# Retention and an ELU feed-forward on one core: w_out loaded in pieces of two rows, strided FFN1 weights, and w_in's last quarter moved ahead of w_out

## The chip, the cores and the metric

The kernel runs on one core of one Trainium2 chip. The metric is the device time of one execution in microseconds. Before the change it is 303.02 us, the median of three runs (302.87 to 303.52). The engines are named as in the profile: PE (TensorE matmuls), PEld (TensorE weight loads), DVE (VectorE), ACT (ScalarE), POOL (GpSimd), SP (SyncE, which issues transfers). A name that ends in q is an engine's issuing side.

## The reference

Eight batches of eight heads, 576 positions, head size 64. Retention (linear attention with decay) is followed by a feed-forward layer with ELU over all 4608 tokens:

```python
scores = scale * np.matmul(q, k.transpose(0, 1, 3, 2))
Dmat = np.where(rel >= 0, gamma[:, None, None] ** rel[None, :, :], 0.0)
ret = scores * Dmat[None, :, :, :]
x = np.matmul(ret, v)                 # laid out as [4608, 512]
h = x @ w_in                          # [512, 2048]
g = np.where(h > 0.0, h, np.exp(np.minimum(h, 0.0)) - 1.0)
out = g @ w_out                       # [2048, 512]
```

The inputs and the output are fp32. The kernel multiplies in bf16.

## The kernel before, in words

**Blocks.** The tokens are cut into items of 256 tokens. Batches 0, 1 and 2 have two items each, and each of these is prepared in two units of four heads (units 0 to 11); later batches are prepared by whole items, and the last 64 positions of each batch are gathered in two tail items, X and Y. The feed-forward works by blocks: blocks 0 to 13 are one item of 256 tokens each, and two blocks of 512 tokens come last.

**A unit.** SP loads its q, k and v (lines 396 to 415). POOL or DVE multiply q and k by powers of the decay (line 522). PE transposes them in two steps, named T4_0 and T4_1 for unit 4 (line 554), and DVE or ACT copy the result out of PSUM. PE computes the scores, DVE masks them (line 888), PE accumulates the running state, and POOL, ACT or DVE cast it (line 841). A last PE step gives this unit's part of x transposed, which ACT or DVE copy to the block's tile xt (line 924).

**FFN1** (line 1025) takes the weights of w_in as the stationary operand and xt as the moving one. One step is two tiles of 128 hidden units by four pieces of the 512 inputs, so eight matmuls of 256 columns, into one of eight PSUM banks. Step p of a block needs hidden columns 256p to 256p + 255 of w_in. ACT computes the exponential (line 1041); for blocks 0 and 1 ACT or DVE then clamp the PSUM bank (lines 1051, 1053), and DVE makes g (line 1063); later blocks use lines 1055 and 1065. **FFN2** (line 1079) takes g as the stationary operand and the rows of w_out as the moving one, 512 columns, 16 hidden tiles in one bank.

**The weights' loads** are issued by POOL, which casts fp32 to bf16 on the way: w_in in five transfers (wi0 and wi1 of 256 columns, wi2, wi3 and wi4 of 512; line 449), w_out in four of 512 rows (wo0 to wo3; line 461). Hidden unit 128f + p stands on partition p of tile f. All these transfers go through one queue. All other loads and the stores go through SP's.

**The order of the work** is fixed when the program is built. Each piece of work is an operation with costs per engine, a rank and the operations it depends on; `Plan.run` (line 67) plays these through in time and writes the instructions of each engine in the order in which it started them. The chip then runs each engine in this order, with waits by semaphore. Lower ranks go first. `AT` (line 216) names operations that the planner doesn't start before a given time, and so chooses the place of the weights' loads among POOL's work; `HOLD` (line 214) puts a memset on POOL ahead of a load, so that SP issues this load and all behind it only after the memset; `RANKS` (line 217) shifts a rank; `VLATE` (line 215) lists items whose v loads come behind both units' q and k. While PE has nothing to do in the plan's first 50 us, the kernel writes matmuls or transposes of a zero tile into the gap (lines 1184 to 1194), about 60 ns each; these stand in the order as well. The costs that the planner gives to PE's retention steps are in `cost_of` (line 933) and in `flush` (line 1019).

Of the kernel before, what the change touches and what calls it, by code (L numbers as in the profile page):

```python
# [17 lines left out]
P = 128  # L18
# [17 lines left out]
class Plan:  # L36
# [6 lines left out]
    def add(self, *a, **kw):  # L43
        op = Op(*a, **kw)
        self.ops.append(op)
        for key in op.use:
            self.users.setdefault(key, []).append(op)
            op.turn += self.owner.get(key, [])
        for cls, key, *_ in op.take:
            self.owner[key] = [op]  # L50
            if cls not in FREE:
                op.turn += self.takers.get(cls, [])
                self.takers[cls] = [op]
        return op
# [140 lines left out]
SW_ENTER = 4.2  # L195
# [3 lines left out]
ISSUE = 0.65  # L199
JOINT = True  # L200
BD_ACT = 0.6
BD_POOL = 0.46
UB_POOL = 0.33
SCALED = 1.06
# [6 lines left out]
EARLY = 6  # L211
PE_TURN = 6
APART = (4, 5)
HOLD = {"ldq4": 14.4, "ldq5": 23.9, "ldv4": 30.1, "ldv6": 24.3, "ldq6": 16.8}
VLATE = ()
AT = {"wi0": 6.9, "wi1": 10.0, "wi2": 7.2, "wi3": 10.0, "wi4": 19.7, "wo0": 18.0, "wo1": 19.0, "wo2": 21.3, "wo3": 27.5, "ex_0_2": 20.36, "st5": 44.96, "cp5_0": 43.84, "cv1": 9.05}
RANKS = {"F2_0_0_8_0": -2}
FREE = ("f", "e", "em", "g", "ot")
SURE = 3
ATT = ((0, 0), (0, 1), (1, 0), (1, 1), (2, 0), (2, 1), (3, 0), (3, 1), (4, 0), (4, 1), "X",  # L220
# [12 lines left out]
def kernel(  # L233
# [9 lines left out]
    nc = tc.nc  # L243
# [18 lines left out]
    pin = tc.keep_in_program_order  # L262

    def mm(*a, **kw):
        return pin(nc.tensor.matmul(*a, **kw))  # L265
# [46 lines left out]
    for c in range(2):  # L312
        for ek in range(2):
            m = mask_u[c * C : (c + 1) * C, ek]
            nc.gpsimd.affine_select(out=m, in_=m, compare_op=ALU.is_ge, fill=0.0, base=-ek, pattern=[[1, 2], [2, C]],
                                    channel_multiplier=-2)
    w_in_sb = const.tile([P, KJ, DF], BF16, name="w_in_sb")
    w_out_sb = const.tile([P, NFT, DM], BF16, name="w_out_sb")

    plan = Plan(SLOTS)  # L320
    add = plan.add
# [4 lines left out]
    def T(cls, key, shape, dt):  # L326
        return (cls, key, shape, dt)
# [7 lines left out]
    items, at, order_of = [], {}, []  # L335
    for n, key in enumerate(ATT):
        it = Work()
# [19 lines left out]
    for i, keys in enumerate(FFN):  # L357
        blk = Work()
# [17 lines left out]
    def load_part(name, dst, src, key, first, shape, cost=(0.9, 32)):  # L376
# [3 lines left out]
        hold = None  # L380
        if first and name in HOLD:
            def emit_h(op):
                pin(alu[op.eng].memset(tiles[key][:, 0, :1], 0.0))  # L383

            hold = add(f"hold{name}", {"POOL": 0.1}, [], emit_h, len(plan.ops) - 1000, take=[T("r", key, shape, FP32)])
            hold.early = HOLD[name]
            first = False
# [8 lines left out]
    def load(it):  # L396
        n = it.n
        shape = [P, 2 * H, D]
        if it.units:
            for u, what in [(u, what) for u in it.units for what in "qkv"] if it.n not in VLATE else \  # L400
                    [(u, what) for u in it.units for what in "qk"] + [(u, "v") for u in it.units]:
# [59 lines left out]
    def load_w_out(i):  # L461
        n0, n1 = W_OUT[i]

        def emit(op):
            pin(nc.gpsimd.dma_start(w_out_sb[:, 4 * n0 : 4 * n1],
                                    moe_w_out[n0 * 512 : n1 * 512, :].rearrange("(f p) n -> p f n", p=P)))

        op = add(f"wo{i}", {"POOL": 0.8}, [], emit, -1000, dma=(2.75 * (n1 - n0), 32 * (n1 - n0), SW_ENTER))
        op.slack = 0.4
        for ft in range(4 * n0, 4 * n1):  # L470
            w_out_ld[ft] = op
# [229 lines left out]
    def state_of(it, c):  # L701
        if it.tail:
            return ("bd", it.b + c, 8)
        return ("bd", it.b, NC * it.T + c) if it.T + c else None

    def ustate_of(u, c):
        return ("s", u.b, 2 * u.T + c, u.w) if u.T + c else None
# [139 lines left out]
    def after_state(it, st, tkey, off):  # L847
        if it.unit:
            return after_state_unit(it, st, tkey, off)
        for c in range(NC):  # L850
# [25 lines left out]
            def emit_b(op, skey=skey, bkey=bkey):  # L876
                pin(copy[op.eng](tiles[bkey], tiles[skey]))  # L877

            bd_op[bkey] = [add(f"bd{it.b}_{cc}", {"POOL": BD_POOL, "ACT": (0.41, BD_ACT), "DVE": (0.3, 1.5)}, [s_op], emit_b,
                               it.rank + 3, take=[T("bd", bkey, [P, HP, D], BF16)], use=[skey])]  # L880
# [21 lines left out]
    def state_keys(it):  # L902
        return [s for s in ([ustate_of(it, c) for c in range(2)] if it.unit else [state_of(it, c) for c in range(NC)]) if s]

    def inter_uses(it):
        return state_keys(it) + ([("qkT", it.n), ("vn", it.n)] if it.unit else [("qkT2", it.n), ("kv", it.n)]) + [("pt", it)]

    def inter_deps(it):
        return [*it.mask, *it.laid, *(op for s in state_keys(it) for op in bd_op[s])]
# [22 lines left out]

    def cost_of(it, parts):
        if it.unit:
            return (0.112 if state_keys(it) and "i" in parts else 0) + 0.24 * sum(p in parts for p in "sv") + \
                0.13 * ("t" in parts)
        t = 0.32 if "i" in parts else 0.0
        return t + 0.26 * sum(p in parts for p in "svt")

    def reserve(op, keys):  # L940
# [19 lines left out]
    def pair_of(key):  # L960
        return [(key, par) for par in range(2)]
# [51 lines left out]
    def flush(it):  # L1013
        xkey = ("x", it)

        def emit(op):
            attend(it, None, xkey, None, 0)

        iv = add(f"iv{order_of.index(it)}", {"PE": (0.22 if it.unit and ustate_of(it, 0) is None else 0.45) + cost_of(it, "iv")}, inter_deps(it), emit, it.rank + 2, use=inter_uses(it))
        reserve(iv, pair_of(xkey))  # L1020
        put_x(it, xkey, iv)

# [2 lines left out]
    def ffn1(blk, p, rank, after):  # L1025
        hkey, ekey, gkey, mkey = ("h", blk.i, p), ("e", blk.i, p), ("g", blk.i, p), ("em", blk.i, p)
        per, first = 512 // blk.w, blk.i < 2
        fts = range(per * p, per * (p + 1))

        def emit(op):  # L1030
            ph, xt = tiles[hkey], tiles["xt", blk.i]
            for f, ft in enumerate(fts):
                for j in range(KJ):
                    mm(ph[:, f * blk.w : (f + 1) * blk.w], w_in_sb[:, j, ft * P : (ft + 1) * P], xt[:, j],
                       start=(j == 0), stop=(j == KJ - 1))

        f1 = add(f"F1_{blk.i}_{p}", {"PE": 0.873 if per == 2 else 0.864}, [*blk.done, *(w_in_ld[ft] for ft in fts)],
                 emit, rank, take=[T("f", hkey, [P, 512], FP32)], use=[("xt", blk.i)], after=after)

        def emit_e(op):  # L1040
            pin(nc.scalar.activation(tiles[ekey], tiles[hkey], AF.Exp))  # L1041

        ex = add(f"ex_{blk.i}_{p}", {"ACT": 0.6}, [f1], emit_e, rank, take=[T("e", ekey, [P, 512], FP32)],
                 use=[hkey], banks=[(hkey, 0)])
        kind = {}

        def emit_m(op):
            ph, e, em = tiles[hkey], tiles[ekey], tiles[mkey]
            kind[0] = "relu" if op.eng == "ACT" or first else "em"
            if op.eng == "ACT":  # L1050
                pin(nc.scalar.activation(ph, ph, AF.Relu))  # L1051
            elif first:
                pin(nc.vector.tensor_scalar_max(ph, ph, 0.0))
            else:
                pin(alu[op.eng].tensor_scalar_add(em, e, -1.0))  # L1055

        md = add(f"md_{blk.i}_{p}", {"ACT": 0.6, "DVE": 0.66 if first else 0.54}, [ex], emit_m, rank,
                 take=[T("em", mkey, [P, 512], BF16)], use=[hkey, ekey], banks=[(hkey, 0)])

        def emit_g(op):  # L1060
            ph, e, g = tiles[hkey], tiles[ekey], tiles[gkey]
            if kind[0] == "relu":
                pin(nc.vector.scalar_tensor_tensor(g, e, -1.0, ph, ALU.add, ALU.min))  # L1063
            else:
                pin(nc.vector.scalar_tensor_tensor(g, ph, 0.0, tiles[mkey], ALU.max, ALU.min))  # L1065

        blk.g[p] = add(f"g_{blk.i}_{p}", {"DVE": 0.69}, [md], emit_g, rank, take=[T("g", gkey, [P, 512], BF16)],
                       use=[hkey, ekey, mkey], banks=[(hkey, 0)])
        return f1
# [60 lines left out]
    for i in range(len(W_OUT)):  # L1130
        load_w_out(i)
    prev = None
    for it in order_of:
        if it.unit and it.early:
            early(it)
            continue
        stretch(prev, it)
        prev = it
        if not it.unit and it.n in APART:
            flush(it)  # L1140
            prev = None
# [8 lines left out]
    for blk in blocks:  # L1150
        base, n = (blk.at + len(blk.its)) * 16 + 1, blk.w // P
# [12 lines left out]
    for op, name in holds:  # L1164
        op.deps.append(named[name])
    for name, t in AT.items():
        if name in named:
            named[name].early = t
    for name, shift in RANKS.items():
        if name in named:  # L1170
# [59 lines left out]
```

## Time and profile before

| what | before |
|---|---|
| median of three runs | 303.02 us (302.87 to 303.52) |
| profiled execution: its own time | 302.71 us |
| its span | 301.0 us |
| PE busy | 294.5 us, 98% of the span, 3845 matmuls |
| PEld busy | 190.4 us, 63% |
| DVE busy | 199.9 us, 66% |
| ACT busy | 164.7 us, 55% |
| POOL busy | 118.4 us, 39% |
| FFN1 matmuls on PE | 1024, 139.6 us |
| FFN2 matmuls on PE | 592, 140.0 us |
| chain that ended last | PE 89%, DMA 5%, POOL 3% |
| hardware queue (SP's loads and stores) | 118704 packets, 45.63 MB |
| software queue (w_in, w_out) | 4752 packets, 4.19 MB as written |

The profile is of one execution. Its span runs from the first to the last instruction; its own time is 1.7 us more. Matmuls overlap, so a matmul's duration is longer than the distance to the next one, and a group's busy time is the time in which at least one of its matmuls ran. The chain that ended last is followed back from the last instruction: at each step to what released it. In a row of the order of time the numbers are start and duration, then engine, line, operation, what it writes and reads, and the count; in brackets stands the idle time of the engine ahead of it and what ended it.

### The profile page before, as it was taken

To read this page: it belongs to the slowest core of one execution; us is meant where nothing else is said; L and a number is where in the kernel's file an instruction comes from. 1 tells how busy PE (TensorE), PEld (TensorE's weight loads), DVE (VectorE), ACT (ScalarE), POOL (GpSimd) and SP (SyncE) were. 2 spreads that over 40 slices of the span, in tenths; PEclk is the share of its full clock that TensorE was granted. 3 is DMA by queue.
4 is the path that set the end of the run, shared out by engine and by line. 5 is a ranking of instruction groups with operands and counts; after the bars stand their busy time and mean duration, and the time that the engine had idled before them with its cause. 6 is when DMAs were issued, how large, how long until landed. Compare 5 with 4: busy or idle time off the path is not lost.

```text
span 301.0 us, 9230 instructions
## 1 busy us (share of the span) xinstructions
PE 294.5 (98%) x3845; PEld 190.4 (63%) x3845; DVE 199.9 (66%) x380; ACT 164.7 (55%) x306; POOL 118.4 (39%) x196
## 2 busy tenths in 40 slices
PE   8998999999999999999999999999999999999995
PEld 5676656758665767677666576767676544444444
DVE  3876664957774687768688557678877667766500
ACT  4466653747653576557446356566666437644311
POOL 4954168756472516358066170835710000000000
PEclk9999999999999999999999999999999999999999
DMA  7999999999998995699999679757231000011131
GB/s 209 278 212 211 222 291 275 265 258 199 254 194 138 280 205 148 178 243 232 250 251 211 169 198 244 190 130 185 58 92 38 37 35 35 2 35 36 43 99 70
DMA packets 123498, 50.41 MB, mean 167 GB/s; under 512 B 83392, under 2 KB 118976, under 8 KB 123456
## 3 DMA queue, kind: packets, MB, share of 16 engines
q1 hardware_dynamic: 118704, 45.63, 63.8%
q0 software_dynamic: 4752, 4.19, 8.7%
q8 instruction: 30, 0.49, 0.7%
q14 instruction: 12, 0.10, 0.1%
HBM read 36.70 MB, written 9.44 MB: 153 GB/s over the span
## 4 chain that ended last, share of the span: by engine, by line
PE 89%; DMA 5%; POOL 3%; SPq 1%; issue 0%; ACT 0%; ACTq 0%
PE f L265 89%; DMA r<-in_k_dram 4%; POOL st L522 2%; DMA r<-in_q_dram 2%; POOL w_in_sb L454 1%; SPq L378 1%; PE f L554 0%; POOL s L841 0%; ACT ot L1102 0%; POOL r L383 0%; ACTq L1102 0%
## 5 line engine op out<-in xcount | busy, mean ns | idle before, releaser
L265 PE MATMUL f<-w_out_sb,g 128*128 128x512 bf16 (+1 forms) x592 | 140.0, 374 | 0.0
L265 PE MATMUL f<-xt,w_in_sb 128*128 128x256 bf16 (+1 forms) x1024 | 139.6, 286 | 0.0
L1041 ACT ACTIVATE e<-f 128x512 f32<-128x512 f32 x144 | 85.7, 596 | 74.0 <-PE f L265 69.2
L265 PEld LDWEIGHTS <-w_in_sb 128*128 128x128 bf16 x1024 | 99.2, 98 | 35.8
L265 PEld LDWEIGHTS <-g 128*128 128x128 bf16 x592 | 56.5, 98 | 52.1
L1055 DVE TENSOR_SCALAR em<-e 128x512 bf16<-128x512 f32 x84 | 42.9, 514 | 39.5 <-ACT e L1041 39.2
L1065 DVE SCALAR_TENSOR_TENSOR g<-f,em 128x512 bf16<-128x512 f32 x84 | 57.1, 688 | 4.8
L1063 DVE SCALAR_TENSOR_TENSOR g<-e,f 128x512 bf16<-128x512 f32 x60 | 40.3, 683 | 12.0 <-ACT f L1051 10.9
L579 POOL CAST kv<-r 128x512 bf16<-128x512 f32 x24 | 14.3, 619 | 57.4 <-issue 57.4
L1102 ACT COPY ot<-f 128x512 f32<-128x512 f32 (+1 forms) x37 | 21.2, 574 | 25.7 <-PE f L265 25.4
L1051 ACT ACTIVATE f<-f 128x512 f32<-128x512 f32 x57 | 33.6, 593 | 0.0
L924 ACT CAST xt<-f 128x512 bf16<-128x512 f32 (+1 forms) x38 | 21.4, 614 | 19.9 <-PE f L265 19.6
L599 POOL TENSOR_TENSOR kv<-r,gq 128x512 bf16<-128x512 f32 x24 | 26.4, 1119 | 2.6 <-DMA r<-in_q_dram 2.6
L599 POOL TENSOR_TENSOR kv<-r,gk 128x512 bf16<-128x512 f32 x24 | 25.2, 1057 | 1.4 <-DMA r<-in_k_dram 1.4
L892 DVE TENSOR_TENSOR pt<-f,mask 128x512 bf16<-128x512 f32 x24 | 15.4, 683 | 9.2 <-PE f L265 9.2
L888 DVE TENSOR_TENSOR pt<-f,mask_u 128x512 bf16<-128x512 f32 x24 | 15.4, 683 | 3.0 <-PE f L265 2.9
L877 POOL CAST bd<-S 128x256 bf16<-128x256 f32 x29 | 11.5, 419 | 11.6 <-DVE S L865 5.9
L522 POOL TENSOR_TENSOR st<-r,gk 128x256 bf16<-128x256 f32 x21 | 13.2, 647 | 4.0 <-DMA r<-in_k_dram 4.0
L865 DVE TENSOR_TENSOR S<-f,S 128x256 f32<-128x256 f32 x30 | 12.7, 422 | 1.9
L522 POOL TENSOR_TENSOR st<-r,gq 128x256 bf16<-128x256 f32 x20 | 12.3, 631 | 4.0 <-DMA r<-in_q_dram 4.0
L265 PE MATMUL f<-T 64*64 64x64 bf16 (+1 forms) x576 | 10.5, 201 | 0.0
L265 PEld LDWEIGHTS <-kv 64*64 64x64 bf16 x704 | 9.5, 104 | 0.0
(65 smaller groups left out, 143.1 us busy)
## 6 DMA issues: line engine op xcount, KB each, us to landing
r<-in_k_dram SPq DMA_DIRECT2D x32, 256.0 KB, 4.2
r<-in_v_dram SPq DMA_DIRECT2D x32, 256.0 KB, 4.6
out_dram<-ot SPq DMA_DIRECT2D x31, 256.0 KB, 2.7
r<-in_q_dram SPq DMA_DIRECT2D x10, 512.0 KB, 5.2
r<-in_q_dram SPq DMA_DIRECT2D x12, 256.0 KB, 4.8
w_out_sb<-in_moe_w_out_dram POOLq DMA_DIRECT2D x4, 512.0 KB, 11.8
w_in_sb<-in_moe_w_in_dram POOLq DMA_DIRECT2D x3, 512.0 KB, 11.7
out_dram<-ot SPq DMA_DIRECT2D x10, 128.0 KB, 2.3
```

The lines of the kernel that those rows point to most:

```text
L265: return pin(nc.tensor.matmul(*a, **kw))
L522: pin(alu[op.eng].tensor_tensor(tiles[key][:, i, e].rearrange("p (y x) d -> p x y d", y=2), raw.rearrange("p (x y) d -> p x y d", y=2), g, ...
L599: pin(alu[op.eng].tensor_tensor(tiles[nkey][:, 2 * i + j].rearrange("p (y x d) -> p x y d", y=2, x=HP), raw.rearrange("p (x y) d -> p x y ...
L888: pin(nc.vector.tensor_tensor(pt, src.rearrange("p (h n) -> p h n", h=2), mask_u.rearrange("p k e r -> p (k e r)").unsqueeze(1).to_broadca ...
L892: pin(nc.vector.tensor_tensor(pt.rearrange("p h s n -> p (h s) n"), src.rearrange("p (h n) -> p h n", n=C), mask.rearrange("p e r -> p (e ...
L924: pin(copy[op.eng](dst, src))
L1041: pin(nc.scalar.activation(tiles[ekey], tiles[hkey], AF.Exp))
L1051: pin(nc.scalar.activation(ph, ph, AF.Relu))
L1055: pin(alu[op.eng].tensor_scalar_add(em, e, -1.0))
L1063: pin(nc.vector.scalar_tensor_tensor(g, e, -1.0, ph, ALU.add, ALU.min))
L1065: pin(nc.vector.scalar_tensor_tensor(g, ph, 0.0, tiles[mkey], ALU.max, ALU.min))
L1102: pin(copy[op.eng](tiles[okey][:, :width], tiles[pkey][:, :width]))
```

## The change

w_out is loaded so that one partition takes two consecutive rows: hidden units 256f + 2p and 256f + 2p + 1 stand on partition p, in tiles 2f and 2f + 1. Each piece of a transfer is then twice as long, and there are half as many. To match, FFN1 takes every second column of a group of 256 columns of w_in as its stationary operand. Step p of a block needs the same columns of w_in as before.

In the tables, w_in's last transfer (wi4) is allowed from 17.7, ahead of w_out's four, no longer behind the first two of them; wi3 and wo1 move by 1.0; item 0 (units 0 and 1) loads its values behind both units' q and k; unit 6's load of q is no longer held; the shifted rank and four delays of operations are gone (unit 1's cast of v, the exponential of block 0's step 2, unit 5's state step and one of its copies). The planner's costs of the two-row transfers and of PE's steps with retention states are changed too; these numbers only shape the order.

```diff
+WO = 2.5
...
-HOLD = {"ldq4": 14.4, "ldq5": 23.9, "ldv4": 30.1, "ldv6": 24.3, "ldq6": 16.8}
-VLATE = ()
-AT = {"wi0": 6.9, "wi1": 10.0, "wi2": 7.2, "wi3": 10.0, "wi4": 19.7, "wo0": 18.0, "wo1": 19.0, "wo2": 21.3, "wo3": 27.5, "ex_0_2": 20.36, "st5": 44.96, "cp5_0": 43.84, "cv1": 9.05}
-RANKS = {"F2_0_0_8_0": -2}
+HOLD = {"ldq4": 14.4, "ldq5": 23.9, "ldv4": 30.1, "ldv6": 24.3}
+VLATE = (0,)
+AT = {"wi0": 6.9, "wi1": 10.0, "wi2": 7.2, "wi3": 11.0, "wi4": 17.7, "wo0": 18.0, "wo1": 20.0, "wo2": 21.3, "wo3": 27.5}
+RANKS = {}
...
-            pin(nc.gpsimd.dma_start(w_out_sb[:, 4 * n0 : 4 * n1],
-                                    moe_w_out[n0 * 512 : n1 * 512, :].rearrange("(f p) n -> p f n", p=P)))
+            pin(nc.gpsimd.dma_start(w_out_sb[:, 4 * n0 : 4 * n1].rearrange("p (f e) n -> p f (e n)", e=2),
+                                    moe_w_out[n0 * 512 : n1 * 512, :].rearrange("(f p e) n -> p f (e n)", p=P, e=2)))
-        op = add(f"wo{i}", {"POOL": 0.8}, [], emit, -1000, dma=(2.75 * (n1 - n0), 32 * (n1 - n0), SW_ENTER))
+        op = add(f"wo{i}", {"POOL": 0.8}, [], emit, -1000, dma=(WO * (n1 - n0), 16 * (n1 - n0), SW_ENTER))
...
-            return (0.112 if state_keys(it) and "i" in parts else 0) + 0.24 * sum(p in parts for p in "sv") + \
+            return (0.056 if state_keys(it) and "i" in parts else 0) + 0.24 * sum(p in parts for p in "sv") + \
                 0.13 * ("t" in parts)
-        t = 0.32 if "i" in parts else 0.0
+        t = 0.07 * len(state_keys(it)) if "i" in parts else 0.0
...
-        iv = add(f"iv{order_of.index(it)}", {"PE": (0.22 if it.unit and ustate_of(it, 0) is None else 0.45) + cost_of(it, "iv")}, inter_deps(it), emit, it.rank + 2, use=inter_uses(it))
+        iv = add(f"iv{order_of.index(it)}", {"PE": (0.28 if it.unit and ustate_of(it, 0) is None else 0.5) + cost_of(it, "iv")}, inter_deps(it), emit, it.rank + 2, use=inter_uses(it))
...
-                    mm(ph[:, f * blk.w : (f + 1) * blk.w], w_in_sb[:, j, ft * P : (ft + 1) * P], xt[:, j],
+                    hidden = slice(2 * P * (ft // 2) + ft % 2, 2 * P * (ft // 2 + 1), 2)
+                    mm(ph[:, f * blk.w : (f + 1) * blk.w], w_in_sb[:, j, hidden], xt[:, j],
                        start=(j == 0), stop=(j == KJ - 1))
```

## The prediction

> **What bounds the kernel now.** I read the page's slices first, then the chain that ended last, then the waits, then PE's order of work up to 60 us, then POOL's, and last each transfer's issue and landing. The slices:
>
> ```profile
> PE   8998999999999999999999999999999999999995
> PEld 5676656758665767677666576767676544444444
> DVE  3876664957774687768688557678877667766500
> DMA  7999999999998995699999679757231000011131
> ```
>
> Each digit is a slice of 7.5 us. PE is full from the fifth slice (30 us) to the last but one, at full clock (PEclk is 9 everywhere). DVE and ACT have room nearly everywhere; DMA is full from the second slice to the thirteenth. So the time is PE's own work plus what PE loses in the first 30 us. The chain says the same and names the place where the loss ends:
>
> ```profile
> 12.99 1.76 POOL st L522 x3
> ...
> 15.05 0.37 SPq L378
> 15.42 0.04 issue
> 15.46 11.62 DMA r<-in_k_dram
> 27.08 0.07 issue
> 27.15 1.19 POOL st L522 x2
> 28.34 0.05 issue
> 28.39 0.29 PE f L554 x2
> 28.67 15.13 PE f L265 x146
> ```
>
> The columns are start, duration, what. The key load of unit 4 takes 11.62 us, POOL scales it, PE transposes it at 28.39, and from there PE never waits until 297.77. The last stretches of PE ahead of that point, start and duration first, and one piece from the middle of the kernel:
>
> ```profile
> 17.93 1.12 PE L265 MATMUL f<-zero 128*128 128x128 bf16 x17
> 18.89 1.04 PE L265 MATMUL f<-xt,w_in_sb 128*128 128x256 bf16 x8
> ...
> 21.90 1.92 PE L265 MATMUL f<-xt,w_in_sb 128*128 128x256 bf16 x16
> 24.26 0.28 PE L554 MATMUL f<-ident,st 128*128 128x128 bf16 x2 [0.44 <-POOL st L522]
> 24.83 0.28 PE L554 MATMUL f<-ident,st 128*128 128x128 bf16 x2 [0.29 <-POOL st L522]
> 24.95 2.78 PE L265 MATMUL f<-xt,w_in_sb 128*128 128x256 bf16 x24
> 27.82 0.28 PE L554 MATMUL f<-ident,st 128*128 128x128 bf16 x2
> 28.39 0.29 PE L554 MATMUL f<-ident,st 128*128 128x128 bf16 x2 [0.28 <-POOL st L522]
> ...
> 100.51 3.66 PE L265 MATMUL f<-xt,w_in_sb 128*128 128x256 bf16 x32
> ```
>
> Eight matmuls are one FFN1 step (two hidden tiles of 128). PE stands at two transposes of unit 4, although FFN1 steps that could run are queued behind them: from 21.90 to 28.50 it is busy 5.51 of 6.60 us, so 1.09 us are lost there.
>
> **The change, part by part.**
>
> *FFN1's weights, every second column.* 1024 matmuls get a strided weight load; 896 have 256 moving columns, 128 have 512. The last row above gives the pitch: (3.66 - 0.27)/31 = 109 ns, 0.27 us being one matmul's duration. The weight load overlaps it. What a contiguous load needs at most is read from the 17 filler matmuls at 17.93, each with a load of its own: (1.12 - 0.22)/16 = 56 ns. So 53 ns of cover are left per FFN1 matmul. No row has a strided load. Lower end: nothing, and not below it, since the pitch follows the moving columns (512 columns take 216 ns, twice 108), not the load. If the load's occupancy doubles, 112 ns shows over 109: 896 x 3 ns = +2.5 us. The far end is the load's whole recorded duration, 98 ns, doubled and uncovered: 896 x (196 - 109) = +78 us. I take 0, since the nearest row is the 56 ns one and even twice that is all but covered; 2.5 us stays for the range.
>
> [...]
>
> *w_out in pieces of two rows.* Four transfers as before, POOL's issue 0.78 us each, with half the packets: 2,048 packets of 1,024 bytes become 1,024 of 2,048. The trace's mean packet takes 60 ns at 512 bytes and 98 at 1,024, so by a straight line 174 at 2,048, against 196 for two: 11% less, 0.3 us of a transfer. The other end: three software transfers that ran alone landed at 29.56, 32.10 and 34.64 us, 2.54 apart; 1.05 MB of fp32 in that time is 413 GB/s, perhaps all there is. Beside the load queue, packets alternate about one for one (140 and 140 per us from 19 to 25 us), so bigger ones take more from it; that could cost the late loads up to 0.3 us per transfer. Either way PE has other work, so 0.
>
> *The last quarter of w_in ahead of w_out.* Transfers of this queue land in order of issue. Before: w_in's fourth at 23.95, then w_out 0 at 27.04, w_out 1 at 29.56, w_in's fifth at 32.10, w_out 2 at 34.64, w_out 3 at 38.20. After, I expect the fifth of w_in at about 27.1, w_out 0, 1, 2 at about 29.6, 32.1 and 34.6, w_out 3 as before (POOL issues it only at 30.20). Who waits? At 28.51 PE has done 8 of the 16 FFN1 steps of the first two blocks; four more need only what landed at 23.95, and then it turns to FFN2 at 32.46 while the fifth transfer comes in. After the change all eight can run: 8 x 0.873 = 7.0 us plus 0.35 for unit 4's scores, so PE is covered to 35.9 without any of w_out, 6 us past its first landing. Nothing gained, nothing lost: 0. The first thing late next would be block 2, whose first FFN1 step starts at 50.28 with 12 matmuls of FFN2 (2.6 us) still in hand; it hangs on the loads from 31 us on, which move by tenths.
>
> *Item 0's values last.* SP issues the same six loads in another order. Landings at 6.33, 7.13 and 7.88 us belonged to v0, q1, k1 and will belong to q1, k1, v0. q1 ends a wait of 1.93 us on POOL, ahead of the first two w_in issues at 8.00. So these may go up to 0.8 us earlier; the first FFN1 step (15.75) follows the landing of the first (15.55) and the second half of xt (ready about 15.6). Software packets begin only at 10.9, at half rate beside the loads, so little of the 0.8 arrives. v0 comes 1.55 us later, and unit 0's half of xt (9.67) has over 4 us in hand. Between 0 and -0.8 I take -0.2.
>
> *What else goes or moves.* The delays on unit 1's cast, one exponential and two steps of unit 5, one rank and a hold of unit 6's load disappear; the planner takes PE's retention steps as 0.01 to 0.1 us cheaper. These change the order in which instructions stand. From 28.5 us on PE has no idle time in the trace (17.82 busy of 17.82 to 50.28, 180.72 of 180.72 to 231), so an exchange of two steps costs nothing unless it brings a wait. Unit 6's load stays behind unit 4's held one in SP's order, so its hold's loss frees nothing. 0, with half a microsecond to either side.
>
> The waits at unit 4's transposes: its hold (14.4) is unchanged, SP issues at 15.05 after POOL's memset, and the load shares the wire with 1,024-byte packets of w_in now as of w_out before. So I leave the 1.09 us where they are.
>
> **The sum.** The profiled execution took 302.71 us for a span of 301.0. 302.71 + 0 + 0 + 0 - 0.2 + 0 = 302.5. The median of the three runs is 303.02, 0.3 above that execution, so the forecast is **302.8 us**. A measurement of this kernel tells about 0.2%, 0.6 us, from no change; faster begins below 302.4 and slower above 303.6.
>
> **Rivals.**
>
> *Neutral as forecast* (38%): 302.2 to 303.9, of which 27% within the 0.2%, 7% below, 4% above. Here also belongs that the pieces of two rows are split again and land as before.
>
> *The early loss shrinks* (31%): another order puts FFN1 steps ahead of unit 4's transposes, or fewer fillers. For it: 1.09 us are lost while steps wait behind, and the 17 fillers from 17.93 delayed a step by 0.5 us after its weights had landed (18.38). Against: hold and ranks of unit 4 stay. 303.0 - 1.1 - 0.5 = 301.4.
>
> *Strided loads show* (11%): a load's occupancy doubles to 112 ns and passes the 109 of a 256-column matmul; from that point each of 896 pays the excess. 303.0 + 2.5 = 305.5. Against it speaks that twice the measured occupancy barely reaches the pitch.
>
> *FFN1 bunches* (20%): without FFN2 between, FFN1 steps follow each other at 0.873 us, while each needs 0.60 (exponential), 0.59 (relu) and 0.69 (gate) on ACT and DVE, 0.94 us when shared evenly, and unit 4's masks and copies (1.28 and 0.84) come on top. Eleven steps from 24.95: 11 x 0.07 + 2.1/2 = 1.8 us behind, two steps. It costs PE only when all 8 PSUM banks are taken, that is when the two engines are some five steps behind or an FFN2 step finds its gate unfinished; then about 1 us, 304.1. Before, ACT stood 2.20 and DVE 2.59 us idle in the FFN2 run at 35 us, so they can catch up.
>
> Faster 7 + 31 = 38%, same 27%, slower 4 + 11 + 20 = 35%. The range reaches from the fast rival to most of the slow ones: 301.2 to 304.9.
>
> **What would show it.** Right: 3,728 packets in the software queue instead of 4,752; FFN1's 32-matmul pieces still 3.66 us; eight FFN1 steps in a row between 28 and 37 us, FFN2 from about 36; the idle 1.09 us around unit 4's transposes still there; PE full to the end. Wrong: pieces of FFN1 longer than 3.7 us (strided loads), PE idle with ACT or DVE as the releaser between 30 and 40 us (bunching), unit 4's transposes without waits (early loss), or PE waiting for block 2 around 50 us, which I gave no price.

## The result and the profile after

The changed kernel takes 315.27 us (median of five, 314.73 to 315.96), the kernel before 303.06 us (302.87 to 303.52). The ratio is 1.040, 95% interval 1.0386 to 1.0414: 12.2 us slower. The forecast was 302.8 us in a range of 301.2 to 304.9, so it missed by far, and on the side of its weaker half.

The profiled execution took 314.73 us for a span of 313.0. Of its page, three of the rows that were shown of before, and the row of the granted clock:

```profile
PE   8917899999999999999999999999999999999995
DVE  3813495476687568777768757676876567766600
PEclk9965999999999999999999999999999999999999
DMA  6993998899999998588999999964622100011131
```

From the sixth slice on the rows are like those of before. Most of the loss is in the third and fourth (15.7 to 31.3 us): PE is nearly idle in the third, DVE in the third too, and in both PE has half of its clock or a little over. The rest is a shorter wait across the end of the fourth. The chain that ended last, same stretch as in the prediction:

```profile
11.92 12.99 DMA w_in_sb<-in_moe_w_in_dram
24.91 0.14 issue
25.05 1.67 PE f L266 x7
26.72 0.29 issue
27.00 5.33 DMA w_in_sb<-in_moe_w_in_dram
32.34 0.05 issue
32.38 2.47 PE f L266 x40
```

Where unit 4's keys stood before, there are now two transfers of w_in, with seven FFN1 matmuls between them, and the second is issued only when these are done. PE's order of work (the last row is for a comparison further down), then POOL's:

```profile
16.76 0.27 PE L266 MATMUL f<-xt,w_in_sb 128*128 128x256 bf16 x1
25.05 1.65 PE L266 MATMUL f<-xt,w_in_sb 128*128 128x256 bf16 x7 [8.02 <-DMA w_in_sb<-in_moe_w_in_dram]
...
30.40 0.42 PE L266 MATMUL f<-xt,w_in_sb 128*128 128x256 bf16 x1
32.38 0.94 PE L266 MATMUL f<-xt,w_in_sb 128*128 128x256 bf16 x7 [1.56 <-DMA w_in_sb<-in_moe_w_in_dram]
...
36.41 1.04 PE L266 MATMUL f<-xt,w_in_sb 128*128 128x256 bf16 x8
```

```profile
27.00 0.81 POOL L456 DMA_DIRECT2D w_in_sb<-in_moe_w_in_dram  x1 [9.49 <-PE f L266]
27.81 1.41 POOL L467 DMA_DIRECT2D w_out_sb<-in_moe_w_out_dram  x2
```

The first FFN1 step (eight matmuls) needs hidden columns 0 to 255, which landed at 14.76. Its first matmul runs at 16.76, its second waits until the fourth transfer of w_in, columns 1024 to 1535, has landed at 24.91. And POOL, which has nothing to wait for in the data, holds the fifth transfer, columns 1536 to 2047, until that FFN1 step is done, with all of w_out behind it. The next FFN1 step repeats it: one matmul, then a wait for the fifth transfer. These are waits that the program has and the data doesn't need.

### The profile page after: what moved, and what is told of

Read it like the earlier page. It is cut to its first block, busy times and chain, and to the rows that moved or that the text cites. A ratio compares the mean times of both kernels' runs of the same rounds, so it can differ in the third digit from the quotient of the medians.

```text
span 313.0 us, 9248 instructions
## 1 busy us (share of the span) xinstructions
PE 297.4 (95%) x3851; PEld 192.9 (62%) x3851; DVE 198.1 (63%) x375; ACT 165.6 (53%) x309; POOL 118.6 (38%) x197
## 3 DMA queue, kind: packets, MB, share of 16 engines
q0 software_dynamic: 3728, 4.19, 8.1%
## 4 chain that ended last, share of the span: by engine, by line
PE 89%; DMA 7%; POOL 2%; SPq 0%; issue 0%; ACT 0%; ACTq 0%
PE f L266 89%; DMA w_in_sb<-in_moe_w_in_dram 6%; DMA r<-in_q_dram 2%; POOL st L524 1%; POOL w_in_sb L456 1%; SPq L380 0%; PE f L556 0%; ACT ot L1105 0%; POOL s L843 0%; ACTq L1105 0%
## 5 line engine op out<-in xcount | busy, mean ns | idle before, releaser
L1058 DVE TENSOR_SCALAR em<-e 128x512 bf16<-128x512 f32 x79 | 40.7, 517 | 40.4 <-ACT e L1044 40.1
L1068 DVE SCALAR_TENSOR_TENSOR g<-f,em 128x512 bf16<-128x512 f32 x79 | 53.6, 688 | 4.3
L1066 DVE SCALAR_TENSOR_TENSOR g<-e,f 128x512 bf16<-128x512 f32 x65 | 43.7, 683 | 12.7 <-ACT f L1054 11.2
L1054 ACT ACTIVATE f<-f 128x512 f32<-128x512 f32 x62 | 36.5, 592 | 0.0
L926 ACT CAST xt<-f 128x512 bf16<-128x512 f32 (+1 forms) x41 | 22.4, 603 | 18.4 <-PE f L266 18.2
L524 POOL TENSOR_TENSOR st<-r,gq 128x256 bf16<-128x256 f32 x19 | 12.2, 657 | 1.8 <-DMA r<-in_q_dram 1.4
L562 DVE COPY T<-f 128x512 bf16<-128x512 bf16 x10 | 4.2, 421 | 12.0 <-PE f L556 11.9
```

The costliest lines, as they stand in the source:

```text
L524: pin(alu[op.eng].tensor_tensor(tiles[key][:, i, e].rearrange("p (y x) d -> p x y d", y=2), raw.rearrange("p (x y) d -> p x y d", y=2), g, ...
L926: pin(copy[op.eng](dst, src))
```

## The experiments

**Theory A:** when the program's waits are made, FFN1's strided read of w_in is taken to overlap transfers that write other columns, so FFN1 waits for other transfers and a transfer waits for FFN1. **Theory B:** the new order and the new tables cost the 12 us. **Theory C:** strided weight loads are slower on the chip. Ratios are to the kernel before on the same chip, with 95% intervals.

**Own tiles.** Each of w_in's transfers writes a tile of its own; the strided read and the whole order stay.

```diff
-    w_in_sb = const.tile([P, KJ, DF], BF16, name="w_in_sb")
+    w_in_own = [const.tile([P, KJ, (n1 - n0) * 256], BF16, name=f"w_in_sb{i}") for i, (n0, n1) in enumerate(W_IN)]
+    w_in_at = {n: (w_in_own[i], (n - n0) * 256) for i, (n0, n1) in enumerate(W_IN) for n in range(n0, n1)}
...
-                    mm(ph[:, f * blk.w : (f + 1) * blk.w], w_in_sb[:, j, hidden], xt[:, j],
+                    own, o = w_in_at[ft // 2]
+                    mm(ph[:, f * blk.w : (f + 1) * blk.w], own[:, j, o + ft % 2 : o + 2 * P : 2], xt[:, j],
```

> The changed kernel, strided weights kept, with each of w_in's five transfers in a tile of its own. Theory A (the strided read of one big w_in tile gives the program waits that the data doesn't need: FFN1 waits for every w_in transfer issued so far, and the next w_in transfer on POOL waits for FFN1): the 8.0 us wait at 16.8 us, POOL's 9.5 us wait and the half-speed clock from 17 to 31 us go, time 302 to 304 us. Theory B (the new order and tables cost the 12 us): 314 to 316. Theory C (strided weight loads are slower on the chip): 305 or more, with FFN1's 32-matmul pieces longer than 3.66 us.

Measured: 303.15 us, ratio 1.0004 (0.9991 to 1.0017). The whole loss is gone. PE's order of work:

```profile
15.73 1.04 PE L266 MATMUL f<-xt,w_in_sb 128*128 128x256 bf16 x8
...
28.15 0.29 PE L557 MATMUL f<-ident,st 128*128 128x128 bf16 x2 [0.92 <-POOL st L525]
28.72 0.28 PE L557 MATMUL f<-ident,st 128*128 128x128 bf16 x2 [0.29 <-POOL st L525]
28.84 1.04 PE L266 MATMUL f<-xt,w_in_sb 128*128 128x256 bf16 x8
...
30.16 6.29 PE L266 MATMUL f<-xt,w_in_sb 128*128 128x256 bf16 x56
36.28 4.05 PE L266 MATMUL f<-w_out_sb,g 128*128 128x512 bf16 x18
```

The first step starts at 15.73 and runs through, and 56 strided matmuls in a row take (6.29 - 0.27)/55 = 109 ns each, as contiguous ones did. Theory A holds as to the waits; B falls, since the order is that of the changed kernel, and C too. PE still stands at unit 4's transposes: 0.92 and 0.29 us in these rows, and 0.19 us at 24.32.

**The stride alone,** on the kernel before:

```diff
-                    mm(ph[:, f * blk.w : (f + 1) * blk.w], w_in_sb[:, j, ft * P : (ft + 1) * P], xt[:, j],
+                    hidden = slice(2 * P * (ft // 2) + ft % 2, 2 * P * (ft // 2 + 1), 2)
+                    mm(ph[:, f * blk.w : (f + 1) * blk.w], w_in_sb[:, j, hidden], xt[:, j],
```

> The kernel before, with FFN1 reading every second column and nothing else changed; w_out stays in its old order, so this kernel pairs hidden units with wrong rows and is read for its time alone. Theory A: the first FFN1 step waits for the fourth transfer of w_in (about 24 us, 7 to 8 us of idle PE) and POOL waits for FFN1 before it issues the fifth, which here has two w_out transfers ahead of it; 310 to 314 us. Theory B: 303. Theory C: 305 to 306, with no wait added.

Measured: 319.55 us, ratio 1.053 (1.0498 to 1.0565), more than theory A said. PE at the first FFN1 step, and POOL:

```profile
26.36 1.65 PE L265 MATMUL f<-xt,w_in_sb 128*128 128x256 bf16 x7 [10.05 <-DMA w_in_sb<-in_moe_w_in_dram]
...
32.71 0.74 POOL L454 DMA_DIRECT2D w_in_sb<-in_moe_w_in_dram  x1 [14.74 <-PE f L265]
```

FFN1's first step waits 10.05 us. In this order two w_out transfers stand ahead of w_in's fifth, and by the time POOL comes to it a second FFN1 step, at 31.38, is among those it waits for; FFN1 waits 5.19 us more, to 38.07. The kind was foreseen, the size not: I had counted the first wait only. With the rest of the change around it, w_in's last quarter ahead of w_out among it, the same stride costs less: 315 us instead of 320.

**The rest without the stride:** the changed kernel with the old line of FFN1 put back (the reverse of the last diff).

> The changed kernel with contiguous weights in FFN1 and everything else as changed; hidden units are paired with wrong rows of w_out, so it is read for its time alone. Theory A: 302 to 304 us, no wait of FFN1 beyond the landing of its own columns, clock 1.0 throughout. Theory B: 314 to 316. Theory C: 302 to 304 as well, which run 1 tells apart.

Measured: 303.19 us, ratio 0.9997 (0.9985 to 1.0009), with the clock at 1.0. No FFN1 step waits for a transfer of other columns; the first runs through:

```profile
14.89 1.04 PE L266 MATMUL f<-xt,w_in_sb 128*128 128x256 bf16 x8
```

**The move alone:** the kernel before with w_in's fifth transfer first.

```diff
-"wi4": 19.7
+"wi4": 17.7
```

> The kernel before with w_in's last transfer allowed from 17.7, so that POOL issues it ahead of w_out's first two, nothing else changed. Theory A and the prediction's step: no change, 302.4 to 303.6 us, the fifth w_in transfer lands about 27 us and w_out 0 about 29.6. Theory B: slower by a good part of the 12 us.

Measured: 303.08 us, ratio 0.9998 (0.9983 to 1.0013). The fifth transfer landed at 27.27 us, w_out's first at 29.81.

**One tile, laid out by transfer.** What is the strided read taken to overlap? Its own range, 256 columns of one piece of the 512 inputs, holds nothing that another transfer writes, so the transfer must be taken as larger than it is. In the big tile a transfer writes one run of columns in each of four pieces, and the pieces are 2048 columns apart. The range from a transfer's first to its last place holds the second and third piece of all columns, and the fourth up to the transfer's own last column. For the transfers behind the first it doesn't hold the first 256 columns of the first piece. So the first matmul would be free and the second not, as in the trace.

```diff
+    w_in_sb = const.tile([P, KJ * DF], BF16, name="w_in_sb")
+    w_in_at = {n: (KJ * 256 * n0, n1 - n0, n - n0) for n0, n1 in W_IN for n in range(n0, n1)}
...
+            pin(nc.gpsimd.dma_start(w_in_sb[:, KJ * 256 * n0 : KJ * 256 * n1].rearrange("p (j n) -> p j n", j=KJ), moe_w_in[:, c].rearrange("(j p) n -> p j n", p=P)))
...
+                    base, wide, n = w_in_at[ft // 2]
+                    o = base + (j * wide + n) * 256
+                    mm(ph[:, f * blk.w : (f + 1) * blk.w], w_in_sb[:, o + ft % 2 : o + 256 : 2], xt[:, j],
```

> The changed kernel with w_in in one tile again, but laid out by transfer: the four pieces of the 512 inputs that one transfer brings stand next to each other on a partition, so the columns that a strided read spans lie inside what one transfer writes. If a strided read is taken to touch everything between its first and last place in the tile, or a transfer everything between its first and last (theory A as I now read it, since the first matmul, with piece 0, did not wait and the second, with piece 1, did): 302.5 to 304 us, no wait on other transfers. If any strided read waits for every transfer into the same tile: 314 to 316 us.

Measured: 303.33 us, ratio 1.0003 (0.9988 to 1.0019). The first step waits only for its own transfer, which landed at 16.16:

```profile
16.21 1.05 PE L266 MATMUL f<-xt,w_in_sb 128*128 128x256 bf16 x8 [0.60 <-DMA w_in_sb<-in_moe_w_in_dram]
```

One tile and a strided read are harmless as long as the ranges of reads and transfers don't cross. Contiguous reads in the big tile (before, and the run without the stride) had no such waits, though their ranges cross in the same way; so it takes the strided read and the crossing ranges together. The rule itself is inferred from these runs; the code that makes the waits isn't shown here.

**Only the fifth transfer apart,** which splits the 12 us:

```diff
-    w_in_sb = const.tile([P, KJ, DF], BF16, name="w_in_sb")
+    w_in_sb = const.tile([P, KJ, 1536], BF16, name="w_in_sb")
+    w_in_last = const.tile([P, KJ, 512], BF16, name="w_in_last")
...
+                    own, o = (w_in_last, 256 * (ft // 2) - 1536) if ft >= 12 else (w_in_sb, 256 * (ft // 2))
```

> The changed kernel with only w_in's fifth transfer in a tile of its own. The wait of POOL for FFN1 and the second wait of FFN1 (1.56 us at 32 us) go, the first wait (8.0 us for the fourth transfer) and the half-speed clock stay. The first wait's work is PE's to do after 25 us: about 6 us of matmuls at least that run 1 had done by then, and half speed for some 6 us: 303.2 + 6 to 10 = 309 to 313 us. If the two waits cost about the same each: 309. If only the waits on POOL mattered: 303 to 305.

Measured: 310.81 us, ratio 1.0268 (1.0247 to 1.0288). So about 7.7 us hang on FFN1's first wait (5.93 us here, the fourth transfer landing at 22.32) and the half clock after it, and about 4.5 us on the wait of POOL for FFN1 and what follows from it. The split is rough: the first wait was 2.1 us shorter than in the changed kernel, where POOL issued the fourth transfer at 11.92 and not at 10.40, and some of the 4.5 us may be that.

**PE kept busy in the wait.** In the changed kernel the granted clock is 0.50 from 17.3 to 31.0 us. Is that a cost of its own?

```diff
             ph, xt = tiles[hkey], tiles["xt", blk.i]
+            for _ in range(145 if (blk.i, p) == (0, 0) else 0):
+                mm(ph[:, :P], zero[:, :P], zero[:, :P], start=True, stop=True)
```

> The changed kernel with 145 matmuls of the zero tile ahead of the first FFN1 step, so that PE is busy instead of idle in the wait for the fourth w_in transfer. The granted clock should then stay at 1.0 to 31 us, where the changed kernel had half speed from 17.3. If the half-speed clock were a cost of its own, six microseconds at half speed are 3 us: 312. If PE would only wait longer for the fifth transfer, which POOL issues when the first step is done: that step takes 0.9 instead of 1.7 us, so 0.8 to 1 us less, 314.2 to 314.5.

Measured: 314.79 us, ratio 1.0394 (1.0371 to 1.0416), against 1.0400 (1.0386 to 1.0414) of the changed kernel: no difference beyond the intervals. PE from the end of the second wait, and the 5 us ahead of it, from 25 to 30 us (busy time of PE, PEld, DVE, ACT, POOL, then clock, DMA share, GB/s):

```profile
31.43 0.94 PE L266 MATMUL f<-xt,w_in_sb 128*128 128x256 bf16 x7 [3.38 <-DMA w_in_sb<-in_moe_w_in_dram]
...
32.55 1.74 PE L266 MATMUL f<-xt,w_in_sb 128*128 128x256 bf16 x8
...
36.88 1.04 PE L266 MATMUL f<-xt,w_in_sb 128*128 128x256 bf16 x8
```

```profile
25.00:30.00 5.00, 2.97 (x73) 2.35 (x70) 2.64 (x5) 1.94 (x4) 2.21 (x3) 1.00 0.50 69
```

The clock stayed at 1.0 through the first wait, the first step ended earlier, and the fifth transfer landed at 31.38 instead of 32.34. Of that one microsecond 0.4 us is the fourth transfer, which landed at 24.54 and not at 24.91; the rest is what the faster PE bought. The second wait, which a transfer ends, grew from 1.56 to 3.38 us, and after it the clock fell to half from 32.7 to 36.2: the eight matmuls at 32.55 took 1.74 us, in the changed kernel (33.50) 1.05. From the end of the second wait to the FFN1 step at 36.88 PE took 5.45 us; in the changed kernel, at full clock, the same instructions took 4.03 us (32.38 to 36.41). So the half clock cost some 0.6 us ahead of the fifth transfer and 1.4 us where PE itself set the pace. This run moved the half clock to another place; it doesn't show what the kernel would take without any.

**Strided loads where nothing covers them:** the fillers of before with every second column of the zero tile as weights.

```diff
-                        mm(spot[:, :P], zero[:, :P], zero[:, :P], start=True, stop=True)
+                        mm(spot[:, :P], zero[:, : 2 * P : 2], zero[:, :P], start=True, stop=True)
```

> The kernel before, in which the filler matmuls of 128 columns take every second column of the zero tile as weights. There the weight load isn't covered by a 256-column matmul. If a strided load takes no longer: 17 of them take 1.12 us as before, 56 ns apart. If its occupancy doubles: 112 ns apart, and the strided loads of FFN1 would show by 3 ns each.

One execution took 303.28 us. The 17 fillers:

```profile
17.96 1.12 PE L265 MATMUL f<-zero 128*128 128x128 bf16 x17
```

The same 1.12 us, 56 ns each: at this step of two, the strided load needed no more of PE here than the contiguous one.

**Unit 4's transposes later,** once in the kernel before, once in the changed kernel with own tiles:

```diff
-"cv1": 9.05}
+"cv1": 9.05, "T4_0": 26.5, "T4_1": 30.2}
```

> The kernel before with unit 4's two transposes not started before 26.5 and 30.2 in the plan, so that three or four FFN1 steps stand ahead of each; nothing else changed. If the 1.09 us that PE stands at them are lost time (the prediction's fast rival): no bracket at the transposes, 301.9 to 302.2 us. If PE's time is made up of something that comes later (block 2 at 50 us, or the gates): 303.0 within 0.3.

Measured: 303.16 us, ratio 1.0008 (0.9987 to 1.0029): nothing. The waits at the transposes are gone, and come back as others:

```profile
32.66 0.42 PE L265 MATMUL f<-T 64*64 64x128 bf16 x16 [0.51 <-DVE T L560]
...
39.73 0.32 PE L265 MATMUL f<-vn,st 64*64 64x64 bf16 x16 [0.89 <-POOL vn L532]
```

Unit 4's scores now stand close behind its transposes and wait for the copy, and its state step comes up before its values (held until POOL's memset) have been loaded and cast.

> The changed kernel with a tile for each w_in transfer and the same two delays. Run 1 lost 1.40 us of PE at unit 4's transposes, 0.19 at the first step and 0.92 and 0.29 at the second; without them 303.15 - 1.4 = 301.8 us, or 303.2 if the time comes back later.

Measured: 301.83 us (301.65 to 302.01), ratio 0.9952 (0.9937 to 0.9968): half a per cent faster than the kernel before, and faster than the changed one. Here all FFN1 steps of the first two blocks can run ahead of FFN2, and PE reaches the state step later:

```profile
30.67 1.91 PE L266 MATMUL f<-xt,w_in_sb 128*128 128x256 bf16 x16
32.51 0.42 PE L266 MATMUL f<-T 64*64 64x128 bf16 x16
...
40.20 0.32 PE L266 MATMUL f<-vn,st 64*64 64x64 bf16 x16 [0.24 <-POOL vn L535]
```

Two FFN1 steps separate transposes and scores, and the wait at the state step is 0.24 us. Which of the tables' differences does it was not taken apart further.

## Why the prediction was wrong, point by point

- **What bounds the kernel: right.** PE's own work plus what PE loses early; all 12 us were lost in the first 33 us. Behind 33.25 us PE is full again, with 276.4 us of busy time left in the changed kernel and 264.4 us before.
- **FFN1's weights, every second column, taken at 0: this step failed.** It asked what a strided load costs PE and answered that correctly (56 and 109 ns, by the filler run and the run with own tiles). It didn't ask what the strided access does to the waits of the program: FFN1's first step waited 8.02 us for columns that it doesn't read, and POOL 9.49 us for FFN1. The term was 12 us: the ratio is 1.040 with the stride in the one tile, 0.9997 without the stride, 1.0004 with the stride in own tiles. None of the rivals and none of the signs listed named this wait. No run shows the doubled occupancy, 112 ns, from which the slow rival's 2.5 us come: the strided filler loads kept to the 56 ns of the contiguous ones.
- **w_out in pieces of two rows, 0: right.** 3,728 packets as foreseen. Landings that ran alone came 2.46 and 2.45 us apart in the run with own tiles (29.36, 31.82, 34.27), against 2.54 before: 0.1 us each, close to the end that said no gain. The straight line for the packets held (its 60 and 98 ns are medians, not means; the median at 2,048 bytes is 173 ns, 174 forecast), but the landings gained less than the 0.3 us that it stood for.
- **The last quarter ahead, 0: right for what it says,** by the run of the move alone. With own tiles the landings were 26.82, 29.36, 31.82 and 34.27 us against the 27.1, 29.6, 32.1 and 34.6 forecast, and FFN2 began at 36.28 against "about 36". In the changed kernel itself the fifth transfer landed at 32.34, later than before, because POOL held it for FFN1.
- **Values last, other tables, -0.2: within the noise.** The run without the stride holds all of these and w_out's pieces: 0.9997 (0.9985 to 1.0009).
- **Unit 4's transposes keep their waits: right** with own tiles (1.40 us). That their loss would be 1.1 us of gain (the fast rival) was wrong on the kernel before, where the time came back at unit 4's scores and values, and right on the version with own tiles (-1.3 us).
- **Bunched FFN1:** 56 matmuls in a row with no wait of PE, so it didn't cost.

## What to carry to other kernels

Where an edit changes the pattern of an access, ask for its effect on the program's waits before its effect on the engine: which reads and which writes of the same tile will now be taken to overlap, and who is queued behind the waiting instruction. The sign in a profile is an instruction that waits for a transfer whose data it doesn't read, or a transfer that waits for a reader of other data. Here a tile for each transfer (303.15 us), or a layout in which ranges don't cross (303.33 us), removed it from the 315.27 us. And a wait that was taken away was worth only what the next late operand left of it: the waits at unit 4's transposes gave nothing on the kernel before (ratio 1.0008) and 1.3 us on the version with own tiles.

## What the runs showed that I had not expected

The first matmul of a step ran and the second waited 8.02 us, though both read columns of one transfer; whether a read was taken to overlap a transfer depended here on its place in the tile. And a wait of 3.38 us, with PE at full clock ahead of it, was followed by about 3.5 us at half clock (32.7 to 36.2), so here an idle stretch cost PE something after its end too: after the 8.02 us wait FFN1's matmuls came 213 ns apart instead of 109. How the half clock follows from the idle time was not shown: it lasted 13.7 us in the changed kernel, and began 0.3 us after PE's last matmul there (at 17.3), but 1.3 us after work had begun again in the run with PE kept busy (at 32.7).
